# Moving the left output product and the second left V pass between the segments of a group in a recurrent-memory kernel

## The chip, the cores and the metric

The kernel runs on one core of one Trainium2 chip. The metric is the device time of one execution in microseconds (us), the lower the better. One profile was taken for each kernel.

## The reference, cut to what matters

The output is `x + A(xn) + B(xn)` with `xn` the layer norm of `x` (2048 rows of 1024). `B` is a dense GELU network and is not touched. `A` goes through 64 segments of 32 rows, one after the other, and carries 8 memory rows from each to the next:

```python
for s in range(n_seg):
    xs = x[:, s * seg_len:(s + 1) * seg_len, :].copy()
    h = jnp.concatenate([mem, xs], axis=1)             # 8 + 32 rows
    q = jnp.einsum('btd,dhe->bhte', h, Wq)             # 32 heads of 128
    k = jnp.einsum('btd,dhe->bhte', h, Wk)
    v = jnp.einsum('btd,dhe->bhte', h, Wv)
    # ... scaled scores, mask, softmax, p @ v ...
    o = jnp.einsum('bhte,hed->btd', o, Wo)
    mem = o[:, :M, :].copy()                           # 8 rows
    outs.append(o[:, M:, :])
```

## The kernel before

A segment has 40 rows, and this kernel gives TensorE tiles of 32 rows. So each segment's own pass takes the 8 memory rows and the first 24 (NX) rows of x. The last 8 (NL) rows, the "left" rows, need no memory for their projections, so they are done for four segments (a group, 4 x 8 = 32 rows) at once, as additional "left half passes" over weight slabs that are passing anyway. The left rows' attention outputs are gathered in `oL`, and their output product is taken once per group.

The weights are 64 slabs of 512 KB. Of these, 43 stay on the chip and 21 are streamed again in every segment through six buffers:

```python
NUNIT = 64
STREAMED = 21
STREAM_BUFS = 6
...
        def unit_done(unit):
            if IS_STREAMED[unit]:
                start_stream()          # the freed buffer is filled again
                ...                     # and a small transfer is issued
```

A half pass is 8 slabs: four matmuls of 512 columns for each slab, in four column tiles, and four more for the left rows where `left` says so. The output product has 16 slabs and eight matmuls of 256 columns for each.

```python
            more = g + 1 < NGRP
            left_k = i4 == 0                                      # K of this group, both halves
            left_q = first or (i4 == 2 and more)                  # Q of the next group
            left_v = first or (i4 == 3 and more), i4 == 0         # V, first and second half
            left_o = i4 == 3                                      # output product
```

So the four segments of a group carry 3, 0, 2 and 3 left half passes (the output product counts two). `qS` keeps the last segment's queries when the next group's replace them in PSUM:

```python
            def keep_q(u):
                nc.vector.tensor_copy(
                    out=qS[:, u, :, :], in_=by_head(qL[:, 4 * u:4 * u + 4, :])[:, :, 3 * NL:4 * NL]
                )
```

The end of a segment, with the load of `resL` (the left rows' residual) in the middle of the output product:

```python
                if n == 7:
                    res = sp.tile([P, 256], BF16, name="res", tag="e")
                    nc.gpsimd.dma_start(out=res[:, :], in_=hr_d[s + 1, :, 256:512])
                    if left_o:
                        resL = late.tile([P, 256], BF16, name="resL", tag="VL1")
                        nc.gpsimd.dma_start(out=resL[:, :], in_=hrL_d[g + 1, :, 256:512])
            ...
            if left_o:
                o_lefts(2)
                nc.vector.tensor_tensor(out=resL[:, :], in0=psXL[:, 0:256], in1=resL[:, :], op=ALU.add)
            if not final:
                put_mem(o_sb, nxt["hT"], trp.tile([P, 4, P], BF16, name="tr"))   # the memory copy, into hr
            nc.vector.tensor_tensor(out=res[:, :], in0=psX[:, 0:256], in1=res[:, :], op=ALU.add)
            # 4 stores of res, and in the fourth segment 16 of resL, go into a queue ("small")
```

`tag` names a buffer: tiles of the same tag share it, and a new one waits for the last reader of the old one. SBUF is full: 512 bytes more in a partition no longer fit.

The softmax here doesn't subtract the row's maximum and nothing guards it: scores larger than these inputs give would overflow.

## Time and profile before

| | before |
|---|---|
| median (3 runs) | 2343.41 us |
| TensorE, busy share | 87% |
| GB/s over the recurrent part, by slices of the span, without the last one | 359 to 406 |
| mean granted TensorE clock | 0.984 |
| longest waits of TensorE's matmuls, us in total | 50.8 for streamed Q slabs, 49.9 "issue" |

How to read the views: a row of a stretch gives its us, each engine's busy us with the count of instructions, the granted TensorE clock (1.00 is full), the transfer engines' busy share, and what they moved in GB/s. A wait row reads "who, tile, line <- whom it waited for: us in total, times, longest". The lines themselves stand in the prediction.

### The profile page before, as it was taken

The page shows a single profiled execution, that of the slowest core. Times are in us where ns is not written, and L with a number is a line of the kernel's source. Part 1 is how long each engine was busy: PE and PEld are TensorE (multiplying, and loading weights), DVE is VectorE, ACT ScalarE, POOL GpSimd, SP SyncE. Part 2 cuts the span into 40 slices and gives each one's busy share as a digit, 9 for nine tenths or more (in the row PEclk, how much of TensorE's full clock was granted, in tenths as well). Part 3 has the DMA queues.
Part 4 walks back from the last instruction along what each step waited for, and adds up shares of the span by engine and source line. Part 5 has one row for each costly group of instructions (what it writes and reads, how often), then busy time and mean ns, then how long its engine had stood idle before and what let it go on. Part 6 is the DMA issues. An engine that isn't in the chain of part 4 may idle for free.

```text
span 2342.5 us, 84620 instructions
## 1 busy us (share of the span) xinstructions
PE 2037.6 (87%) x37779; PEld 1052.9 (45%) x37779; DVE 698.9 (30%) x1922; ACT 516.9 (22%) x1221; POOL 372.7 (16%) x745
## 2 busy tenths in 40 slices
PE   7999999788888888888888888888888888888885
PEld 3444444344444544444444444444444444444443
DVE  6574753122222222222222222222222222222221
ACT  5261432121212121211121211111111111111121
POOL 0000000023121212121212121212121212121212
PEclk9999999999999999999999999999999999999998
DMA  9521126899999999999999999999999999999995
GB/s 326 186 68 47 39 67 256 331 400 372 405 376 404 383 399 374 403 369 389 377 405 367 388 366 404 365 402 367 406 372 404 368 399 361 399 370 403 375 405 225
DMA packets 266410, 792.03 MB, mean 338 GB/s; under 512 B 55996, under 2 KB 71132, under 8 KB 266045
## 3 DMA queue, kind: packets, MB, share of 16 engines
q1 hardware_dynamic: 243004, 769.66, 85.2%
q0 software_dynamic: 22464, 15.92, 2.2%
q8 instruction: 295, 4.83, 0.8%
q10 hardware_dynamic: 576, 1.05, 0.1%
q14 instruction: 71, 0.57, 0.1%
HBM read 772.83 MB, written 29.88 MB: 343 GB/s over the span
## 4 chain that ended last, share of the span: by engine, by line
PE 50%; DMA 40%; issue 4%; DVE 3%; ACT 2%; POOL 1%; DVEq 0%; ACTq 0%; POOLq 0%; SPq 0%
DMA u<-Wc_Q 24%; PE acc L536 18%; PE ps L358 8%; PE acc L676 8%; PE ps L405 6%; DMA u<-Wc_O 5%; DMA u<-Wc_V 4%; DMA u<-Wc_K 3%; PE av L654 2%; DMA resL<-hrL_d 2%; PE tr L493 2%; PE ps L438 2%; PE av L660 1%; DVE natL L564 1%; DVE pr L642 1%
## 5 line engine op out<-in xcount | busy, mean ns | idle before, releaser
L536 PE MATMUL acc<-u,hr 128*32 128x512 bf16 x12288 | 955.6, 385 | 128.7 <-DMA u<-Wc_Q 54.9
L536 PEld LDWEIGHTS <-hr 128*32 128x32 bf16 x12288 | 315.5, 96 | 469.7 <-issue 224.4
L536 PE MATMUL acc<-u,hrL 128*32 128x512 bf16 x3072 | 300.1, 383 | 4.3 <-issue 1.3
L559 ACT CAST nat<-acc 128x512 bf16<-128x512 f32 x256 | 149.8, 585 | 543.1 <-PE acc L536 504.8
L676 PEld LDWEIGHTS <-oT 128*32 128x32 bf16 x8192 | 210.5, 98 | 103.4 <-issue 80.9
L676 PE MATMUL acc<-u,oT 128*32 128x256 bf16 x4096 | 189.5, 277 | 27.0 <-issue 14.2
L564 DVE CAST natL<-acc 128x512 bf16<-128x512 f32 x224 | 152.5, 687 | 173.8 <-PE acc L536 173.8
L676 PE MATMUL acc<-W_O,oT 128*32 128x256 bf16 x4096 | 177.6, 283 | 30.4 <-issue 30.2
L358 PE MATMUL ps<-u 128*128 128x512 bf16 x896 | 195.8, 382 | 2.6 <-ACT u L282 2.6
L194 POOL DMA_DIRECT2D hr<-hr_d x63 | 35.0, 555 | 1009.6 <-PE acc L536 584.6
L778 POOL DMA_DIRECT2D out_dram<-res x256 | 129.4, 512 | 365.5 <-DVE res L774 362.3
L571 DVE COPY kT<-tr 128x512 bf16<-128x512 bf16 x128 | 54.4, 425 | 329.5 <-PE tr L493 329.5
L405 PE MATMUL ps<-u 128*128 128x512 bf16 x672 | 147.0, 379 | 0.0
L358 PEld LDWEIGHTS <-u 128*128 128x128 bf16 x896 | 88.0, 98 | 109.1 <-issue 4.5
L785 POOL DMA_DIRECT2D out_dram<-resL x256 | 127.9, 505 | 50.0 <-DMA out_dram<-resL 22.1
L628 ACT ACTIVATE pr<-sm 128x224 bf16<-128x224 f32 x128 | 45.7, 357 | 405.2 <-PE sm L623 337.3
L583 DVE COPY qT<-tr 128x512 bf16<-128x512 bf16 x128 | 54.4, 425 | 261.0 <-PE tr L493 261.0
L654 PEld LDWEIGHTS <-natL 32*128 32x128 bf16 x2048 | 78.8, 91 | 84.0 <-issue 50.3
L669 DVE CAST oT<-av 128x256 bf16<-128x256 f32 x128 | 54.4, 425 | 199.6 <-PE av L660 197.4
L536 PEld LDWEIGHTS <-hrL 128*32 128x32 bf16 x3072 | 84.2, 97 | 65.4 <-issue 11.3
L654 PE MATMUL av<-pr,natL 32*128 32x40 bf16 x2048 | 95.0, 177 | 17.3 <-DVE pr L642 9.5
L493 PEld LDWEIGHTS <-nat 128*128 128x128 bf16 x1024 | 57.9, 98 | 103.8 <-issue 60.1
(100 smaller groups left out, 1810.5 us busy)
## 6 DMA issues: line engine op xcount, KB each, us to landing
u<-Wc_K SPq DMA_DIRECT2D x384, 512.0 KB, 6.9
u<-Wc_Q SPq DMA_DIRECT2D x384, 512.0 KB, 7.3
u<-Wc_O SPq DMA_DIRECT2D x320, 512.0 KB, 7.3
u<-Wc_V SPq DMA_DIRECT2D x256, 512.0 KB, 6.6
u<-in_B_w_dram SPq DMA_DIRECT2D x16, 448.0 KB, 5.3
u<-in_B_w_dram SPq DMA_DIRECT2D x14, 512.0 KB, 10.7
u<-in_A_Wv_dram SPq DMA_DIRECT2D x12, 512.0 KB, 7.9
u<-in_A_Wk_dram SPq DMA_DIRECT2D x10, 512.0 KB
```

Of the source, the lines that this page charges most:

```text
L358: nc.tensor.matmul(ps[:, :].rearrange("p (s t) -> p s t", t=SEG), lhsT=w1_sb[fb // 14 * 8 + kt][:, (fb % 14) * P:(fb % 14 + 1) * P], rhs=x ...
L405: nc.tensor.matmul(ps[:, :], lhsT=gts[fc // 4][:, fc % 4, t * P:(t + 1) * P], rhs=w2_sb[fc // 2][:, fc % 2, cs], start=(fc == 0), stop=(fc ...
L493: nc.tensor.transpose(dst[:, c, :], nat[:, c * P:(c + 1) * P], ident[:, :])
L536: nc.tensor.matmul(acc[32 * j:32 * j + 32, :], lhsT=lhs[:, i, :], rhs=t[:, 512 * j:512 * j + 512], start=(i == seq[0]), stop=(i == seq[-1] ...
L559: nc.scalar.copy(out=nat[:, :], in_=ps[:, :])
L564: nc.vector.tensor_copy(out=nat[:, :], in_=psL[:, :])
L571: nc.vector.tensor_copy(out=st["kT"][:, :, :], in_=by_head(tr[:, :, :]))
L583: nc.vector.tensor_copy(out=st["qT"][:, :, 0:32], in_=by_head(tr[:, :, :]))
L654: nc.tensor.matmul(oV[:, b, c, :], lhsT=V[q, c * P:(c + 1) * P], rhs=prA[q, c, :], start=(c == 0), stop=False, skip_group_check=True, tile ...
L676: nc.tensor.matmul(acc[32 * jq:32 * jq + 32, 0:256], lhsT=lhs[i // 4][:, i % 4, 2 * u + k, :], rhs=t[:, 1024 * k + 256 * jq:1024 * k + 256 ...
L778: small.append(lambda o=o, r=res[32 * jq:32 * jq + NX, :]: nc.gpsimd.dma_start(out=o, in_=r))
L785: small.append(lambda o=o, r=r: nc.gpsimd.dma_start(out=o, in_=r))
```

## The change

Its intent is two left half passes in each segment, 2, 2, 2, 2 instead of 3, 0, 2, 3. The second left V goes from the first segment to the fourth. The left output product goes from the fourth to the second, and then covers the last four segments up to that one. To make this possible, `resL` leaves the buffer of VL1 for that of `qS`, and is loaded earlier. `keep_q(0)` and the transposes behind it go a little later, and stores are issued at once. The core, with cuts (`...`):

```diff
-            left_v = first or (i4 == 3 and more), i4 == 0
-            left_o = i4 == 3
+            left_v = first or (i4 == 3 and more)
+            left_o = i4 == 1 or final
+            og, slot = divmod(s + 2, GRP)
 ...
-                    at[5] = [lambda: turn_qL(st["natL"], 0)]
-                    ...
-                    qS = sp.tile([P, 2, 16, NL], BF16, name="qS")
-                    at[5].insert(0, lambda: keep_q(0))          # sixth slab of the first V pass
 ...
+            at = {1: [sums]}
+            if left_q and not first:
+                qS = sp.tile([P, 2, 16, NL], BF16, name="qS")
+                at[3] = [lambda: keep_q(0)]                     # fourth slab of the second K pass
+                at[5] = [lambda: turn_qL(st["natL"], 0)]
+            psK1, psK1L = half_pass("K", 1, left_k, at)
 ...
+                def load_resL():
+                    st["resL"] = sp.tile([P, 256], BF16, name="resL", tag="qS")
+                    nc.gpsimd.dma_start(out=st["resL"][:, :], in_=hrL_d[og, :, 256:512])
 ...
+                at[3].append(load_resL)
-            psV1, psV1L = half_pass("V", 1, left_v[1], at)
+            psV1, psV1L = half_pass("V", 1, left_v, at)
 ...
-                        small.append(lambda o=o, r=r: nc.gpsimd.dma_start(out=o, in_=r))
+                            nc.gpsimd.dma_start(out=out_flat[row:row + NL, cs], in_=resL[p0:p0 + NL, :])
```

More of the change, by code (lines that the diff above doesn't have):

```diff
@@ L311, in turn_R @@
             for i in range(4):
-                rows = R_n[ttg * P + i * SEG:ttg * P + (i + 1) * SEG, :].rearrange("t (j c) -> t j c", j=4)
-                dst = hr_d[4 * ttg + i + 1, :, 256:512].rearrange("(j t) c -> t j c", j=4)
-                dstL = hrL_d[ttg + 1, :, 256:512].rearrange("(j t) c -> t j c", j=4)[NL * i:NL * i + NL, :, :]
-                for o, r in ((dst, rows), (dstL, rows[NX:SEG, :, :])):
+                seg = 4 * ttg + i
+                rows = R_n[seg * SEG:(seg + 1) * SEG, :].rearrange("t (j c) -> t j c", j=4)
+                pairs = [(hr_d[seg + 1, :, 256:512].rearrange("(j t) c -> t j c", j=4), rows)]
+                og, slot = divmod(seg + 2, GRP)
+                for sl in (slot, slot ^ 2) if seg in (0, 1, NSEG - 2, NSEG - 1) else (slot,):
+                    dst = hrL_d[og, :, 256:512].rearrange("(j t) c -> t j c", j=4)[NL * sl:NL * sl + NL, :, :]
+                    pairs.append((dst, rows[NX:SEG, :, :]))
+                for o, r in pairs:
                     if small is None:
@@ L506 @@
         qL = qlp.tile([P, 8, P], BF16, name="qL")
-        kL, VL, oL = [None] * 2, [None] * 2, [None] * 2
+        kL, VL = [None] * 2, [None] * 2
+        oL = [late.tile([P, 4, 4, 32], BF16, name=f"oL{u}") for u in range(2)]
+        for t in oL:
+            nc.vector.memset(t[:, :, :, :], 0.0)
         for s in range(NSEG):
@@ L565, in left_out, with left_values @@
                 return nat
+            def left_values(u, ps):
+                VL[u] = left_out(ps, f"VL{u}", late)
             def turn_k(nat):
@@ L665, in values @@
                     st["oT", u] = sp.tile([P, 4, 4, 32], BF16, name="oT", tag="db"[u])
-                    if i4 == 0:
-                        oL[u] = late.tile([P, 4, 4, 32], BF16, name=f"oL{u}")
                 cp = nc.vector.tensor_copy if r else nc.scalar.copy
                 cp(out=st["oT", u][:, 2 * r:2 * r + 2, :, :], in_=oV[:, :, :, 0:32])
-                cp(out=oL[u][:, 2 * r:2 * r + 2, :, NL * i4:NL * i4 + NL], in_=oV[:, :, :, 32:40])
+                cp(out=oL[u][:, 2 * r:2 * r + 2, :, NL * slot:NL * slot + NL], in_=oV[:, :, :, 32:40])
             def o_product(unit, t, lhs, acc, seq):
@@ L698 @@
                 at[2].append(lambda: st.update(natL=left_out(psQL, "d")))
-                at[5] = [lambda: turn_qL(st["natL"], 0)]
                 if first:
-                    at[5].append(lambda: q_left(0))
-                else:
-                    qS = sp.tile([P, 2, 16, NL], BF16, name="qS")
-                    at[5].insert(0, lambda: keep_q(0))
-            psV, psVL = half_pass("V", 0, left_v[0], at)
+                    at[5] = [lambda: turn_qL(st["natL"], 0), lambda: q_left(0)]
+            psV, psVL = half_pass("V", 0, left_v, at)
             st["V"] = left_out(psV, "b")
             if first:
-                VL[0] = left_out(psVL, "VL0", late)
-            psK1, psK1L = half_pass("K", 1, left_k, {1: [sums]})
+                left_values(0, psVL)
+            at = {1: [sums]}
[4 more added lines that the diff above has]
+            psK1, psK1L = half_pass("K", 1, left_k, at)
             natk1 = rows_out(psK1, "d")
@@ L716 @@
                 at[4].insert(0, lambda: turn_kL(st["natL"], 1))
+            if left_v and not first:
+                at[6].append(lambda: left_values(0, psVL))
             psQ1, psQ1L = half_pass("Q", 1, left_q, at)
             natq1 = rows_out(psQ1, "b")
-            if left_v[0] and not first:
-                VL[0] = left_out(psVL, "VL0", late)
             at = {3: [lambda: turn_q(natq1)], 6: [lambda: scores(1)]}
@@ L734, in o_lefts @@
                         o_product(unit, unit_tile(unit), oL, psXL, O_LEFT_SEQ)
+                def load_resL():
+                    st["resL"] = sp.tile([P, 256], BF16, name="resL", tag="qS")
+                    nc.gpsimd.dma_start(out=st["resL"][:, :], in_=hrL_d[og, :, 256:512])
                 at.setdefault(1, []).append(lambda: o_lefts(0))
-            psV1, psV1L = half_pass("V", 1, left_v[1], at)
+                at[3].append(load_resL)
+            psV1, psV1L = half_pass("V", 1, left_v, at)
             st["V"] = left_out(psV1, "a")
-            if left_v[1]:
-                VL[1] = left_out(psV1L, "VL1", late)
+            if first:
+                left_values(1, psV1L)
             if not final:
@@ L745 @@
             at = {1: [sums], 4: [lambda: values(1, 0)], 6: [lambda: values(1, 1)]}
+            if left_v and not first:
+                at[6].append(lambda: left_values(1, psV1L))
             if left_q and not first:
@@ L750 @@
             psX = accp.tile([P, 512], F32, name="acc")
-            resL = None
             for n, unit in enumerate(O_UNITS):
@@ L762 @@
                     nc.gpsimd.dma_start(out=res[:, :], in_=hr_d[s + 1, :, 256:512])
-                    if left_o:
-                        resL = late.tile([P, 256], BF16, name="resL", tag="VL1")
-                        nc.gpsimd.dma_start(out=resL[:, :], in_=hrL_d[g + 1, :, 256:512])
             if not final:
@@ L770 @@
                 o_lefts(2)
+                resL = st["resL"]
                 nc.vector.tensor_tensor(out=resL[:, :], in0=psXL[:, 0:256], in1=resL[:, :], op=ALU.add)
@@ L776 @@
             for jq in range(4):
-                o = out_flat[s * SEG:s * SEG + NX, 256 * jq:256 * jq + 256]
-                small.append(lambda o=o, r=res[32 * jq:32 * jq + NX, :]: nc.gpsimd.dma_start(out=o, in_=r))
+                cs = slice(256 * jq, 256 * jq + 256)
+                nc.gpsimd.dma_start(out=out_flat[s * SEG:s * SEG + NX, cs], in_=res[32 * jq:32 * jq + NX, :])
             if left_o:
-                rows_o = out_flat[g * GRP * SEG:(g + 1) * GRP * SEG, :].rearrange("(i t) d -> i t d", t=SEG)
                 for jq in range(4):
-                    for i in range(GRP):
-                        o = rows_o[i, NX:SEG, 256 * jq:256 * jq + 256]
-                        r = resL[32 * jq + NL * i:32 * jq + NL * i + NL, :]
-                        small.append(lambda o=o, r=r: nc.gpsimd.dma_start(out=o, in_=r))
+                    cs = slice(256 * jq, 256 * jq + 256)
+                    for sl in range(GRP):
+                        row = (GRP * og - 2 + sl) * SEG + NX
+                        if s - GRP < row // SEG <= s and row >= 0:
+                            p0 = 32 * jq + NL * sl
+                            nc.gpsimd.dma_start(out=out_flat[row:row + NL, cs], in_=resL[p0:p0 + NL, :])
             if not final:
```

## The prediction

> **What bounds the kernel now.** I read the page from its second part, because a mean over the span hides the stages. The first seven of the 40 slices are the dense part, which the diff hardly touches. After them run 64 recurrent segments, which stream 21 of their 64 weight slabs (512 KB each) in every segment.
>
> ```profile
> DMA  9521126899999999999999999999999999999995
> GB/s 326 186 68 47 39 67 256 331 400 372 405 376 404 383 399 374 403 369 389 377 405 367 388 366 404 365 402 367 406 372 404 368 399 361 399 370 403 375 405 225
> ```
>
> The transfer engines look full everywhere, yet the rate swings between about 365 and 405 GB/s: something regular takes a tenth of it away. Segments go in groups of four, because work for the "left" 8 rows of four segments is batched, as extra "left half passes". One half pass is 8 slabs on TensorE. The segment ends are the copies that put the memory into hr; I cut one group at them. The columns are the stretch, its us, busy us by engine with counts, granted clock, DMA share and GB/s.
>
> ```profile
> 797.20:825.40 28.20, 25.85 (x572) 14.80 (x568) 8.50 (x24) 5.55 (x15) 11.65 (x23) 1.00 1.00 378
> 825.40:853.40 28.00, 22.38 (x476) 11.07 (x476) 6.03 (x19) 5.55 (x15) 3.12 (x6) 1.00 1.02 404
> 853.40:882.00 28.60, 26.05 (x548) 13.31 (x548) 7.43 (x22) 5.55 (x15) 3.11 (x6) 0.94 1.02 395
> 882.00:914.40 32.40, 28.04 (x648) 15.56 (x648) 6.82 (x21) 5.55 (x15) 3.64 (x7) 1.00 1.00 386
> ```
>
> By the code these carry 3 (K, K, one V), 0, 2 (Q, Q) and 3 (one V, and the output product, which is worth two) left half passes. The second has none and still takes 28.0 us at 404 GB/s: there the transfers are the bound. The fourth is the long one. Where does the rate go? The same view in short stretches across the group's end, at 914.4:
>
> ```profile
> 898.00:906.00 8.00, 7.48 (x198) 4.43 (x193) 2.82 (x8) 2.00 (x6) 0.55 (x1) 1.00 1.02 403
> 910.00:914.40 4.40, 2.40 (x58) 1.33 (x52) 0.50 (x3) 0.37 (x1) 0.00 (x0) 1.00 0.88 327
> 914.40:918.40 4.00, 3.92 (x71) 1.87 (x72) 0.35 (x2) 0.59 (x1) 3.36 (x7) 1.00 0.58 165
> 918.40:922.40 4.00, 3.86 (x63) 1.63 (x65) 2.00 (x5) 0.58 (x1) 2.22 (x6) 1.00 0.95 323
> ```
>
> There is one hole. All six stream buffers are full, since the fourth segment's TensorE work has outlasted the stream, and the next segment starts with slow K passes. Missing bytes against 404 GB/s: 77 x 4.4 + 239 x 4 + 81 x 4 = 1.62 MB, or 4.0 us. The group moves 28.2 x 378 + 28 x 404 + 28.6 x 395 + 32.4 x 386 = 45.8 MB, which at 404 GB/s takes 113.3 us, against 117.2 us: a gap of 3.9 us. So the hole is the whole of what better balance can win: about 15 x 3.9 = 58 us, 2.5%.
>
> Part of the hole is a wait on VectorE, in the wait view from 500 us on (total us, times, longest):
>
> ```profile
> DVE resL L771 <- DMA resL<-hrL_d: 59.2, 10, 7.0
> ```
>
> The add into resL waits for its load, and the memory copy, which the next segment needs, stands behind it.
>
> **What the Trainium skill says.** "DMA: Bandwidth & Descriptors", section Bandwidth, measures 425 GB/s for a 16 MB transfer and puts the port ceiling at 435; this trace shows 403 to 414 in full stretches, so 404 is a fair ceiling with the small transfers in. The same page, Anatomy of one DMA, says that the fixed cost of a transfer from GpSimd is mostly the wait for the write's receipt, 2.0 us in its fit. The trace agrees in kind but not in size: the 4 KB stores of resL take a median of 5.4 us to land under this load (1.5 at least). "Perfetto Trace Analysis", Optimization Strategy, says that regimes with different most-contended engines can gain from interleaving. The table above is that case. "TensorE: Matmul & The Clock Gate", part 3, says that column-tiled matmuls overlap in the array. Here groups of four start 0.21 to 0.22 us apart although one lasts 0.39:
>
> ```profile
> 1006.02 0.39 PE L536 MATMUL acc<-u,hrL 128*32 128x512 bf16 x4
> 1006.24 0.39 PE L536 MATMUL acc<-u,hr 128*32 128x512 bf16 x4
> 1006.45 0.39 PE L536 MATMUL acc<-u,hrL 128*32 128x512 bf16 x4
> ```
>
> So a left half pass costs 8 x 0.215 = 1.72 us of TensorE, and the left output product 3.44.
>
> **The change, part by part.** (1) V of the second half moves from the first segment to the fourth, the output product from the fourth to the second: 3, 0, 2, 3 becomes 2, 2, 2, 2. The instruction order adds only 128 matmuls (one output product, in the last segment), 3.4 us. The first segment, with three half passes, takes 28.2 us, of which TensorE's wait view gives 1.0 to streamed slabs; so three cost about 27.2 us and two about 25.5 (estimate). Four such make 102 us, below the 113.3 us of transfers: the kernel becomes bound by transfers throughout, and the hole should close.
>
> (2) resL is loaded during the V pass, not in the output product: the wait above (6.0 us idle on VectorE in this group, of which the next segment feels some 1.4) goes.
>
> (3) resL shares its buffer with qS, no longer with VL1. In the third segment keep_q(0) writes qS, so it must wait until all 16 stores of resL have landed. The instruction order shows that wait on keep_q, and a wait for VectorE on the qL transposes behind it. This is the new cost. How late do they land? The trace of before has the same 4 + 16 stores after its fourth segment, which ends at 914.4:
>
> ```profile
> 915.04 2.02 POOL L778 DMA_DIRECT2D out_dram<-res  x4 [6.10 <-DVE res L774]
> 917.05 1.99 POOL L785 DMA_DIRECT2D out_dram<-resL  x4
> 919.49 1.00 POOL L785 DMA_DIRECT2D out_dram<-resL  x2 [0.44 <-DMA out_dram<-res]
> 924.30 2.00 POOL L785 DMA_DIRECT2D out_dram<-resL  x4 [0.37 <-DMA out_dram<-resL]
> 926.97 1.14 POOL L785 DMA_DIRECT2D out_dram<-resL  x2 [0.67 <-DMA out_dram<-resL]
> ```
>
> The last is issued 13.2 us into the segment and lands near 18.4 (+5.4 is the median; the packets of 14 groups end at 18.4 on average). The author put keep_q(0) later, to the fourth slab of the second K pass, but TensorE gets to its transposes (two slabs on) 11.9 us into a third segment, averaged over 14 of them in the trace. So TensorE stands still for about 7 us in every third segment.
>
> (4) Stores go out at once instead of through the small queue. GpSimd issued them back to back before too, as shown; nothing changes but the tail. The last segment stores 8 pieces of resL instead of 16: 8 x 0.505 = 4.0 us, and about 0.6 us for the earlier resL.
>
> **What is hidden.** A TensorE stall costs nothing while the stream still has empty buffers. Six buffers of 512 KB at 404 GB/s are 7.8 us. By the time of the stall one or two may already be full, since the left output product lets the stream run ahead; so of 7 us, 0 to 1.5 us leave the transfers idle. After it TensorE starts with full buffers and at once meets the second left Q pass: 8 slabs take 3.44 us and transposes, against 8/3 x 1.3 = 3.5 us of transfers, so the stream pauses again for about 1 us. I take 1.9 us of idle in all: 115.2 us per group, 2.0 saved. Sum: 15 x 2.0 = 30 us in the groups, near 5 in the tail, and 2 to 3 for the first groups, whose s=2 stall is shorter (8 stores): 2343.4 - 37 = 2306.
>
> **Rivals.** A: the stall is wholly hidden (buffers are empty when it comes), and the hole closes: 58 + 5 saved, 2280. For it: by the trace the second segment is starved and so leaves the stream little ahead. Against it: the 7 us are close to all that the buffers hold. B: the stall takes the place of the hole in full, because the stores are slower under a stream that is now always saturated, or TensorE comes to it with several buffers full: 3.5 to 4 us idle per group, 2335 to 2340. For it: 5.4 us to landing is ruled by load, and up to eight stores are out at once, so each us more adds two over 16 stores. C: instruction fetches or small loads limit the rate: TensorE has unexplained stalls ("issue") of 1 to 1.7 us in output passes. These are there before as well and should cancel.
>
> **Range and chances.** 2306 us with 2276 to 2334 for 8 in 10: the low end is rival A at a slightly better rate, the high end near rival B. Faster by over 2% needs under 2297, that is 2.8 of the 3.9 us in each group: 0.34. Slower by over 2% would need a stall that outruns the buffers by 7 us: 0.02.
>
> **What would show it.** Right: four segments of nearly equal half passes, the resL wait gone, the 165 GB/s hole at the group's start gone, GB/s in the 40 slices near 395 and flat. For the stall: a new row "qL waits for qS" on TensorE of about 15 x 7 us, VectorE's qS waiting for out_dram<-resL, the third segment the longest (34 us) and the fourth and first short (24 to 26). The prediction is wrong if that row is missing or under 3 us each (then A), or if the rate in the third segment falls under 360 (then B).

## The result, and the profile after

| | before | after |
|---|---|---|
| median of 4 runs | 2346.33 us | 2482.95 us |
| lowest, highest | 2343.22, 2351.43 | 2467.62, 2486.84 |
| clock in the profiled run | 0.984 | 0.952 |

The ratio is 1.0568 (95% interval 1.0518 to 1.0618): slower by 5.7%, outside the predicted range. All ratios here are the mean time of one kernel's runs over that of the runs of the kernel before in the same rounds, so not quite the ratio of the medians quoted. The experiments ran on four chips, so the ratios are the safer comparison.

The page's second part, of the changed kernel (clock, busy share of the transfers in tenths, GB/s, in 40 slices):

```profile
PEclk9999999999898999998999899999998999999898
DMA  9422028999898989898989899989898999999996
GB/s 327 162 63 56 30 84 308 403 362 399 308 397 306 396 317 399 324 391 308 397 329 390 309 388 338 395 320 385 334 383 317 359 359 373 350 348 350 336 382 269
```

The swing has not gone. It has become deeper, to 306 GB/s, and the clock row now dips; in the kernel before, that row was nines up to the last slice. One group, cut at the copies into hr:

```profile
1204.10:1232.40 28.30, 25.06 (x548) 13.12 (x540) 8.02 (x22) 5.56 (x15) 3.11 (x6) 1.00 1.02 397
1232.40:1263.80 31.40, 25.40 (x604) 14.35 (x604) 6.35 (x21) 5.56 (x15) 4.16 (x8) 1.00 1.01 389
1263.80:1299.60 35.80, 25.92 (x548) 13.30 (x548) 7.44 (x23) 5.55 (x15) 11.11 (x22) 0.86 0.80 285
1299.60:1329.40 29.80, 25.29 (x548) 13.06 (x552) 7.15 (x21) 5.56 (x15) 3.11 (x6) 1.00 1.03 406
```

TensorE is nearly equally busy in all four, 25.1 to 25.9 us: the balance was reached. Yet the third segment takes 35.8 us. The waits that this was expected to show, from 500 us on:

```profile
PE qL L497 <- DVE qS L612: 100.5, 14, 8.5
DVE qS L612 <- DMA out_dram<-resL: 96.7, 13, 8.3
```

The stall is where the prediction put it, and as long: 100.5 us in 14 segments, 7.2 us each. The row of resL waiting for its load is gone from the list. The third segment and the end of the second, in short stretches:

```profile
1258.00:1263.80 5.80, 3.53 (x114) 2.85 (x106) 0.49 (x3) 0.37 (x1) 0.28 (x1) 1.00 0.90 328
1263.80:1267.80 4.00, 3.91 (x72) 1.86 (x74) 0.36 (x2) 0.59 (x1) 3.35 (x7) 1.00 0.81 275
1267.80:1274.80 7.00, 6.22 (x130) 2.90 (x130) 2.72 (x7) 1.52 (x4) 4.65 (x11) 1.00 1.01 386
1274.80:1278.80 4.00, 0.00 (x0) 0.00 (x0) 0.00 (x0) 0.00 (x0) 2.00 (x5) 0.65 1.03 405
1278.80:1282.30 3.50, 0.00 (x0) 0.00 (x0) 0.10 (x1) 0.00 (x0) 0.00 (x0) 0.50 0.33 126
1282.30:1286.30 4.00, 3.83 (x36) 1.40 (x35) 0.12 (x1) 0.59 (x1) 0.00 (x0) 0.51 0.36 129
1286.30:1294.30 8.00, 7.71 (x193) 4.05 (x190) 2.55 (x8) 2.00 (x6) 0.56 (x1) 1.00 0.79 245
```

Three things are to be seen. The hole after the left output product is still there (328 and 275 GB/s), one boundary earlier in the group than before. In the stall (no TensorE work at all) the transfers go on for 4 us and then run dry (126). And after the stall they stay low for 12 us, while TensorE is busy: for the first 4 us its clock is 0.51, then 1.00. TensorE's list in order of time shows that clock in the distance between groups of four matmuls:

```profile
1284.67 0.64 PE L547 MATMUL acc<-u,hr 128*32 128x512 bf16 x4
1285.10 0.64 PE L547 MATMUL acc<-u,hrL 128*32 128x512 bf16 x4
1285.52 0.64 PE L547 MATMUL acc<-u,hr 128*32 128x512 bf16 x4
...
1286.97 0.39 PE L547 MATMUL acc<-u,hrL 128*32 128x512 bf16 x4
1287.18 0.39 PE L547 MATMUL acc<-u,hr 128*32 128x512 bf16 x4
```

They start 0.42 to 0.43 us apart at first and 0.21 later. Against 404 GB/s, the bytes missing from the dry part of the stall to the segment's end are 278 x 3.5 + 275 x 4 + 159 x 8 + 49 x 5.3 (that last stretch ran at 355) = 3.6 MB, or 8.9 us. Over 15 groups that is 134 us, and the kernels differ by 137.

### The profile page after: what moved, and what is told of

The parts are those of the page before. It is cut to its first block, busy times and chain, and to the rows that moved or that the text cites. A ratio compares the mean times of both kernels' runs of the same rounds, so it can differ in the third digit from the quotient of the medians.

```text
span 2485.1 us, 84860 instructions
## 1 busy us (share of the span) xinstructions
PE 2067.6 (83%) x37907; PEld 1063.8 (43%) x37907; DVE 701.0 (28%) x1925; ACT 517.4 (21%) x1221; POOL 374.2 (15%) x748
## 4 chain that ended last, share of the span: by engine, by line
DMA 35%; PE 35%; issue 5%; DVE 3%; ACT 2%; POOL 2%; DVEq 0%; ACTq 0%; POOLq 0%; SPq 0%
PE acc L547 17%; DMA u<-Wc_Q 16%; PE acc L688 9%; DMA out_dram<-res 5%; DMA out_dram<-resL 5%; PE av L668 2%; DMA res<-hr_d 2%; PE tr L497 2%; DMA u<-Wc_O 2%; DMA u<-Wc_V 2%; DMA u<-Wc_K 1%; POOL out_dram L795 1%; PE av L674 1%; POOL out_dram L803 1%; DVE pr L656 1%
## 5 line engine op out<-in xcount | busy, mean ns | idle before, releaser
L547 PE MATMUL acc<-u,hr 128*32 128x512 bf16 x12288 | 979.4, 395 | 113.7 <-DMA u<-Wc_Q 36.4
L547 PE MATMUL acc<-u,hrL 128*32 128x512 bf16 x3072 | 310.0, 396 | 9.4 <-ACT nat L570 7.8
L688 PE MATMUL acc<-W_O,oT 128*32 128x256 bf16 x4096 | 180.9, 288 | 30.4 <-issue 30.2
L547 PEld LDWEIGHTS <-hrL 128*32 128x32 bf16 x3072 | 87.1, 100 | 84.9 <-issue 30.4
L497 PE MATMUL qL<-ident,natL 128*128 128x128 bf16 x128 | 16.2, 266 | 112.6 <-DVE qS L612 108.8
```

The costliest lines, as they stand in the source:

```text
L497: nc.tensor.transpose(dst[:, c, :], nat[:, c * P:(c + 1) * P], ident[:, :])
L547: nc.tensor.matmul(acc[32 * j:32 * j + 32, :], lhsT=lhs[:, i, :], rhs=t[:, 512 * j:512 * j + 512], start=(i == seq[0]), stop=(i == seq[-1] ...
L688: nc.tensor.matmul(acc[32 * jq:32 * jq + 32, 0:256], lhsT=lhs[i // 4][:, i % 4, 2 * u + k, :], rhs=t[:, 1024 * k + 256 * jq:1024 * k + 256 ...
```

## The experiments

The means by segment below were worked out by cutting each trace at the copies into hr, without the first group.

| kernel | median, us | ratio to before | 1st | 2nd | 3rd | 4th | group |
|---|---|---|---|---|---|---|---|
| before | 2346.3 | 1 | 28.5 | 27.9 | 28.8 | 32.2 | 117.4 |
| after | 2482.95 | 1.0568 | 28.9 | 32.5 | 36.4 | 29.0 | 126.8 |
| e1_staged_store | 2346.17 | 1.0002 | 28.5 | 32.3 | 28.2 | 28.6 | 117.6 |
| e2_before_early_resL | 2341.79 | 0.9985 | 28.8 | 28.0 | 28.6 | 31.6 | 117.0 |
| e5_V1_in_first | 2338.04 | 0.9972 | 29.3 | 31.9 | 27.9 | 27.7 | 116.8 |
| e3_filler_in_stall | 2450.45 | 1.0445 | 28.5 | 32.5 | 34.6 | 28.7 | 124.3 |
| e7_half_the_stores | 2408.63 | 1.0256 | 28.3 | 32.3 | 32.8 | 28.9 | 122.3 |
| e6_half_left_product | 2326.87 | 0.9917 | 28.0 | 31.5 | 28.9 | 28.2 | 116.6 |
| e8_wide_left_product | 2319.53 | 0.9885 | 27.8 | 31.5 | 28.4 | 28.2 | 115.9 |
| v1_split_left_product | 2335.28 | 0.9949 | 31.2 | 27.8 | 28.9 | 28.7 | 116.6 |
| e10_no_left_product | 2301.16 | 0.9816 | 28.5 | 28.4 | 29.0 | 29.0 | 114.9 |
| e9_five_buffers | 2445.23 | 1.0410 | 30.6 | 33.3 | 29.4 | 29.9 | 123.1 |
| v2_wide_left_product | 2320.19 | 0.9875 | 29.3 | 30.4 | 28.5 | 27.5 | 115.7 |

e6, e8 and e10 compute wrong left rows; their result still passed the comparison on the chip, whose tolerance is coarse beside the attention's share of the output. e7 leaves half of the left rows unwritten. The third segment of the last group has no left Q pass and so no stall; it is in the means of the 3rd column.

### e1: take the cause of the stall away

The buffer cannot get a tag of its own, since SBUF is full. So resL goes out in one store to a scratch tensor, and the 16 pieces are put in place from there.

```diff
+    oL_d = dram.tile([NGRP + 1, P, 256], BF16, name="oL_d")
 ...
+            if left_o:
+                nc.gpsimd.dma_start(out=oL_d[og, :, :], in_=resL[:, :])
 ...
-                            nc.gpsimd.dma_start(out=out_flat[row:row + NL, cs], in_=resL[p0:p0 + NL, :])
+                            nc.gpsimd.dma_start(out=out_flat[row:row + NL, cs], in_=oL_d[og, p0:p0 + NL, :])
```

> The changed kernel, but resL goes to a scratch tensor in one store, and the 16 pieces are put in place from there, so its buffer is free after one landing (about 8 us into the third segment, before keep_q needs it at about 10.6). Theory S (the loss is the stall on the shared buffer and what follows it: per group 4.6 us of idle transfers in the stall and 4.6 after it, by the 1-us rate table of the changed kernel; balance itself wins nothing, because the hole of 4.0 us after the left output product only moved): the row of qL waiting for qS falls from 7.5 us per group to under 0.5, and the time to 2483 - 15 x 9.2 = 2345, ratio to before 0.99 to 1.01. Rival B (balance works as I predicted, the hole goes): 2280 to 2300, ratio 0.98 or less. Rival O (direct stores or the output product in the second segment are slow in themselves): stays over 2390, ratio over 1.02.

Measured: 2346.17 us, ratio 1.0002 (0.9984 to 1.0020). The wait of qL for qS is 1.1 us in all. So the whole 5.7% is the stall and what follows it, and all the rest of the change, the balance included, is worth nothing within 0.2% (e1's own extra store is in this sum and was not measured apart). The stretches around the end of a second segment show why (it ends at 1218.1):

```profile
1212.20:1218.10 5.90, 3.60 (x118) 2.91 (x106) 0.53 (x3) 0.37 (x1) 0.34 (x1) 1.00 0.94 341
1218.10:1222.10 4.00, 3.95 (x72) 1.90 (x76) 0.33 (x1) 0.59 (x1) 2.69 (x6) 1.00 0.90 297
1222.10:1229.10 7.00, 6.37 (x133) 3.05 (x133) 2.86 (x8) 1.52 (x4) 4.90 (x10) 1.00 1.01 386
```

It is the hole of before, at the segment that now has the output product, although that segment has no other left work and the next begins with plain K passes.

### e2: the early load of resL alone

The kernel before, with `load_resL` in the V pass of the fourth segment, into the buffer of qS (free there).

> The kernel before, with resL loaded during the V pass instead of the output product (into qS's buffer, whose last reader is by then done and whose next writer comes three segments later, so no stall). Takes the early load alone. Theory S: the wait of the memory copy behind the resL add (about 1.4 us per group) goes, but part of it is under the same hole, so 10 to 20 us faster, ratio 0.991 to 0.996. Rival H (the hole is made by the output product alone and the wait is hidden in it): no change, ratio 0.998 to 1.002.

Measured: 2341.79 us, ratio 0.9985 (0.9969 to 1.0002). resL no longer waits for its load, but the gain, if there is one, is about 4 us, less than the 10 to 20 expected. The whole interval lies above theory S's 0.991 to 0.996, so theory S fell as it was put; the interval also reaches 1, so a gain is not shown, and more than 7 us is excluded. That fits a wait that was mostly inside the hole.

### e5: where the left V stands

```diff
-            psV1, psV1L = half_pass("V", 1, left_v, at)
+            psV1, psV1L = half_pass("V", 1, i4 == 0, at)
```

> As e1_staged_store, but the left V of the second half stays in the first segment: 3, 2, 2, 1 left half passes instead of 2, 2, 2, 2. Theory S (where V stands hardly matters, because only the time of the left output product fills the stream buffers): within 0.5% of e1_staged_store. Rival B (equal loads are what counts): slower than e1_staged_store by 1.7 us per group, 25 us, 1.1%.

Measured: 2338.04 us, 0.3% under e1. Loads of 3, 2, 2, 1 do as well as 2, 2, 2, 2 (the intervals, 0.9944 to 1.0001 and 0.9984 to 1.0020, overlap). Equal loads by segment are not what counts.

### e3: the clock apart from the stall

```diff
+                def filler():          # into an unused PSUM tile, never read
+                    av = avp.tile([P, 2, 512], F32, name="av")
+                    t = res_tiles["K", 1, 1]
+                    for n in range(32):
+                        for j in range(4):
+                            nc.tensor.matmul(
+                                av[32 * j:32 * j + 32, 0, :], lhsT=hT[:, 1, :], rhs=t[:, 512 * j:512 * j + 512],
+                                start=True, stop=True, tile_position=(0, 32 * j),
+                            )
+
+                at[4] = [filler]
                 at[5] = [lambda: turn_qL(st["natL"], 0)]
```

> The changed kernel with 32 groups of four matmuls (6.9 us, into an unused PSUM tile, never read) in front of the transposes that wait for qS, so TensorE works through most of the stall instead of standing still. Results stay right. Theory C (the idle stall drops TensorE's granted clock to 0.5 for about 4 us after it, and that costs 2 us per group): the clock stays at 1.0 after the stall, mean clock back near 0.98, and the time falls by about 30 us to 2450, ratio 1.045. Rival N (after the stall the stream, not the clock, sets the pace): the time stays within 10 us of 2483 or rises.

Measured: 2450.45 us, mean clock 0.986. Useless work in the stall makes the kernel 32 us faster than leaving TensorE idle, 2.2 us per group. The stretches from the start of a third segment:

```profile
1254.60:1265.40 10.80, 10.71 (x205) 4.92 (x209) 3.08 (x9) 2.10 (x5) 7.52 (x16) 1.00 0.93 343
1265.40:1272.90 7.50, 6.67 (x124) 3.58 (x117) 0.00 (x0) 0.00 (x0) 2.49 (x5) 1.00 0.73 285
1272.90:1276.90 4.00, 3.20 (x56) 1.53 (x55) 0.65 (x2) 0.58 (x1) 0.00 (x0) 1.00 0.34 120
1276.90:1284.90 8.00, 7.63 (x214) 4.31 (x208) 2.25 (x7) 2.49 (x8) 0.56 (x1) 1.00 0.91 294
```

The clock stays at 1.00, but the transfers still run dry and stay low. The remaining 104 us over e1, 7.0 us per group, are no matter of the clock. (The filler does not lengthen the wait much: the transposes come 19.1 us into a third segment on average, against 18.7 in the changed kernel and 11.6 in e1.) The Trainium skill states the clock's rule ("TensorE: Matmul & The Clock Gate", Part 1): a TensorE that is idle for a window of about 3.4 us is throttled to half its clock, and needs as long of work to get it back. After 7.2 us of standing still the clock is 0.51 for 4 us, and the low stretches of the traces last 3.41, 6.83 or 10.24 us. But 3.4 us of idle time is no limit here: in the kernel before, none of its matmuls waits for more than 2.7 us between 500 and 2300 us, and yet its clock is halved 14 times there, for 3.41 us each. My prediction left the clock out.

### e7: half the stores

```diff
-                    for sl in range(GRP):
+                    for sl in range(2):
```

> The changed kernel with 8 of the 16 pieces of resL stored per group (half of the left rows are not written: wrong result on purpose). By the pace of the stores before (0.68 us each) the last of 8 lands near 12.5 to 13 us into the third segment, so TensorE waits about 2 us instead of 7.5. Theory S (a stall costs only what the full stream buffers cannot cover,[...]): of the 137 us lost more than three quarters come back, 2350 to 2375 us, ratio 1.00 to 1.015. Rival L (loss is proportional to the stall): 137 x 2/7.5 remain, 2383, ratio 1.016 or more.

Measured: 2408.63 us, ratio 1.0256 (1.0214 to 1.0297). TensorE's wait for qS:

```profile
PE qL L497 <- DVE qS L612: 47.4, 14, 5.8
```

The stall is 3.4 us in the mean, not the 2 that I expected, and 62 us of the loss remain, 4.2 us per group. Theory S fell here: far less than three quarters came back. The sum looks proportional, as rival L has it (3.4 / 7.2 x 137 = 65), but this is in part luck, since the clock's share did not shrink with the stall. Theory S had also taken it that so short a stall leaves the clock alone. It doesn't. After a stall of 3.1 us, which ended at 1126.3:

```profile
1125.90:1129.60 3.70, 3.26 (x32) 1.39 (x35) 0.22 (x1) 0.59 (x1) 0.00 (x0) 0.54 1.03 396
```

In all 14 third segments the clock is halved for a time, although in 7 of them no wait of the matmuls is longer than 3.3 us. TensorE works at half clock for 5.2 us in each of them on average, against 4.9 in the changed kernel and 0.9 in e3. If that costs the 2.2 us per group of the changed kernel, some 2 us of the 4.2 are left for the stall of 3.4 itself (an estimate). So the buffers cover up to about 1.4 us of the short stall, and next to nothing of the long one: 7.0 us of cost, with the clock held, for 7.2. A run of e7 with the clock held was not made.

### e6 and e10: how much of the hole is the left output product

In both, only some of the 16 units of the left product are taken, on e1: in e6 the five streamed ones and the last three, in e10 the last one.

```diff
+        O_LEFT = [], [unit for unit in O_UNITS if IS_STREAMED[unit]], O_UNITS[-3:]     # e6
+        O_LEFT = [], [], O_UNITS[-1:]                                                  # e10
```

> e1_staged_store with 8 of the 16 units of the left output product (wrong result on purpose): takes 1.72 us of TensorE out of the second segment and nothing else. Theory H (the hole of about 4 us of idle transfers comes from the left output product standing in one piece at the end of a segment, and it is what six buffers cannot cover): the hole shrinks by as much as is taken out or more, 1.7 to 3.5 us per group, 2294 to 2320 us, ratio 0.978 to 0.989. Rival T (the hole is the chain at the segment's end or the resL add, not the product): within 10 us of e1_staged_store, ratio over 0.996.

> e1_staged_store with 1 of the 16 units of the left output product (wrong result on purpose): the second segment has then almost no left work, 2, 0, 2, 2. Theory H (the hole at the end of the second segment is made by the left output product): all of it goes, 113 to 114 us per group, 2285 to 2305 us, ratio 0.974 to 0.982; the low rates at the second segment's end and the third's start (under 350 GB/s) rise to about 380. Rival T (chain at the segment's end, output transfers, instruction fetches of the main product): over 2320, ratio over 0.988.

Measured: e6 2326.87 us, outside the expected 2294 to 2320 (1.3 us per group for 1.72 us of matmuls); e10 2301.16 us, 45 us under e1's median, or 3.0 us per group for 15 x 0.215 = 3.2 us of matmuls. These matmuls come with waits: in e1 the whole product takes 5.0 us on average, from the first matmul of each of its pieces to the next piece of other work. So e10 takes out some 4.7 us and wins 3.0. Work in this place costs most of its length, although the segment's transfers take longer than its TensorE work. In e10 the hole is gone, at the same place as above (a second segment ends at 1189.3):

```profile
1183.30:1189.30 6.00, 4.18 (x127) 3.02 (x119) 1.07 (x4) 0.86 (x3) 0.53 (x1) 1.00 1.03 400
1189.30:1193.30 4.00, 3.88 (x67) 1.92 (x67) 0.42 (x1) 0.59 (x1) 2.40 (x5) 1.00 1.03 406
1193.30:1200.30 7.00, 6.69 (x133) 3.02 (x131) 2.52 (x7) 1.52 (x4) 4.36 (x10) 1.00 1.03 410
```

### e8: the same columns with half the instructions

On e1, the left product takes two halves of 512 columns for each head instead of four quarters of 256 (even heads in partitions 0 to 63, odd ones in 64 to 127, which are not added up: wrong).

> e1_staged_store with the left output product in 512-wide matmuls, 4 per unit instead of 8 (wrong result on purpose; the same columns stream through TensorE, with half the instructions). Theory H (columns): no change, within 10 us of e1_staged_store, ratio 0.996 to 1.004. Rival F (part of the hole is TensorE waiting for instructions, the row acc waits for issue with 1.7 to 2.8 us in that segment): 1 to 2 us per group less, 2316 to 2331, ratio 0.987 to 0.994.

Measured: 2319.53 us, 27 us under e1, with nearly unchanged matmul time (a unit beside the main product takes 0.219 us in e1 and 0.216 here, medians from its first matmul to the next instruction). So the number of instructions has a part in it. TensorE's "issue" row for the output products, of e1 first:

```profile
PE acc L689 <- issue: 55.1, 44, 2.6
```

and of e8, where the main product has L702:

```profile
PE acc L702 <- issue: 34.4, 33, 2.0
```

Summed over every row in which TensorE's matmuls wait for "issue", it is 75.6 us in e1 and 62.3 in e8. That explains half of the 27 us at most; the other half stays open. The Trainium skill ("Runtime: NRT & Kernel Launch", Instruction fetch mechanics) says that instructions are fetched in 16 KiB blocks by an own queue, and that crossing a block is mostly hidden. e1's trace has this queue with 296 packets of 16 KB; TensorE's 75814 instructions are 296 blocks of 256, the page's size of a block. Between 500 and 2300 us, 50 of its "issue" waits last over 0.5 us (70.3 us in all), and every one of them ends 1.26 to 1.63 us after one of these packets has ended, where 7 in 100 moments taken at random lie 1.2 to 1.7 us behind one. So these waits end with a fetch, and beside a saturated stream fetches are not hidden here. That the stream is what makes them late is not shown.

### v1: the left product cut in two

Five streamed units and three at the end stay in the first segment, the other eight go into the Q and V passes of the second, which has no other left work.

```diff
+        DEFER = [unit for unit in O_UNITS[:-3] if not IS_STREAMED[unit]]
+        NOW = [], [unit for unit in O_UNITS if IS_STREAMED[unit]], O_UNITS[-3:]
 ...
+            split = s > 0 and i4 == 0
+            left_o = split or s == 1 or final
+            og, slot = divmod(s + 3, GRP)
```

> A version meant to beat both (right result). The left output product is cut in two: in the first segment of a group only the 5 streamed units beside the main product and 3 at the end, the other 8 units (1.72 us) in the Q and V passes of the second segment, which has no other left work. V as in the changed kernel (fourth), keep_q where it was before, resL kept from the first to the second segment, where nothing else needs its buffer. Theory H: no stall, and the hole shrinks from 4 us to 0 to 1.5: 114 to 115.5 us per group, 2290 to 2315 us, ratio 0.977 to 0.987. Rival B' (any uneven load, here 3, 1, 2, 2 half passes, brings its own hole): 2335 to 2350, ratio 0.996 to 1.003.

Measured: 2335.28 us, ratio 0.9949 (0.9913 to 0.9984). It is correct and a little faster than before, and a miss against 2290 to 2315, at the lower end of rival B': its first segment, with two left K passes and half of the product, takes 31.2 us and has a hole of its own (253 GB/s at the lowest just after its end, in 1 us slices, mean of 14 groups).

### e9: the size of the window

```diff
-STREAM_BUFS = 6
+STREAM_BUFS = 5
```

> e1_staged_store with five stream buffers instead of six (one more slab stays where the sixth was; the same slabs are streamed). Theory W (what counts is how much TensorE work stands within the window of the stream buffers, some 18 of 64 slabs, not within a segment): every hole grows by what one buffer holds, 1.3 us or more per group, and others open: 2366 to 2410 us, ratio 1.008 to 1.027. Rival (the window does not matter as long as a segment's work is under its transfer time): within 0.4% of e1_staged_store.

Measured: 2445.23 us, 99 us over e1 (96 by the ratios), more than expected. Every segment gets longer, by 1.0 to 2.1 us, while no segment's work or bytes have changed. So the number of buffers sets how far TensorE and the transfers hold each other up. How much of it is the window and how much the shorter queue of transfers in flight, this run doesn't tell.

### v2: a version that beats both

e5 with the wide left product made right: a copy to SBUF, then eight matmuls with parts of the identity add the odd and even heads in the next segment's first K pass, in front of one staged store.

```diff
+                def fold(natXL=natXL, resL=resL, og=og, s=s):
+                    psS = accp.tile([P, 512], F32, name="acc")
+                    for k in range(2):
+                        for jq in range(4):
+                            q = 64 * k + 32 * (jq // 2)
+                            nc.tensor.matmul(
+                                psS[32 * jq:32 * jq + 32, 0:256], lhsT=ident[:, q:q + 32],
+                                rhs=natXL[:, 256 * (jq % 2):256 * (jq % 2) + 256],
+                                start=(k == 0), stop=(k == 1), tile_position=(0, 32 * jq),
+                            )
+                    nc.vector.tensor_tensor(out=resL[:, :], in0=psS[:, 0:256], in1=resL[:, :], op=ALU.add)
```

> A version meant to beat both (right result): e5_V1_in_first with the left output product in 512-wide matmuls (4 per unit instead of 8, even heads in partitions 0 to 63 and odd heads in 64 to 127), folded by 8 matmuls of 256 columns in the next segment's first K pass, then one staged store. Theory F (the instruction stream is part of the hole: e8 won 27 us against e1 with it): 2305 to 2320 us, ratio 0.982 to 0.989. Rival: the fold and the copy in front of it (0.7 us on VectorE, 0.2 us on TensorE) cost what the wide matmuls win: ratio 0.995 to 1.0.

Measured: 2320.19 us, ratio 0.9875 (0.9854 to 0.9897): 1.2% faster than before. The hole at the end of its second segment (1198.5) is smaller, with 399 and 346 GB/s where e1 had 341 and 297:

```profile
1192.60:1198.50 5.90, 4.57 (x122) 3.28 (x120) 0.77 (x4) 0.37 (x1) 0.53 (x1) 1.00 1.03 399
1198.50:1202.50 4.00, 3.97 (x76) 2.00 (x76) 1.33 (x3) 0.58 (x1) 2.57 (x5) 1.00 0.96 346
```

v1 and v2 passed the comparison on the chip. It is coarse, since e6, e8 and e10 passed it too.

## Why the prediction was wrong

- **The stall was right** in its place, its cause, its chain of waits and its length: "about 7 us in every third segment", measured 7.2. (Its list of stores leaves out two rows, with 4 of the 16.) The shared buffer of qS and resL is the cause; e1 takes it away and the 137 us with it.
- **"Six buffers of 512 KB at 404 GB/s are 7.8 us [...] so of 7 us, 0 to 1.5 us leave the transfers idle"** is the step that cost most. I took 1.9 us of idle per group in all; the stall alone cost 7.0 with the clock held (e3 against e1) and 9.1 without, and the hole of 4 us came on top. The transfers ran on for 4 us, not 7.8: some buffers were already full or in use. And the buffers that the stall fills are then missing for what follows. In e1 the stream carries about 400 GB/s through the passes after this point (1 us slices, mean of 14 groups), where after a stall it carries 129 and then 245. So a stall of 7.2 us is not hidden but counts nearly one for one; of the 3.4 us in e7 some 2 remain once the clock's share is taken off (an estimate). That the full buffers are the reason is my reading of those rates; the costs themselves are measured.
- **The clock was not in the prediction.** The stall leaves TensorE at half its clock for the first 4 us of work, 2.2 us per group more (e3), and stalls of 3 us did so too (e7).
- **"Four such make 102 us, below the 113.3 us of transfers: the kernel becomes bound by transfers throughout, and the hole should close"** failed as well. The 102 us were right (101.7 busy in the group shown), the loads became equal, and the hole stayed: 1.0002 for e1, and e5 with unequal loads is no slower. The first and fourth segments took 28.9 and 29.0 us, not the 24 to 26 expected. Sums over a segment of 28 us don't tell, because TensorE and the stream are tied together over six buffers, some 8 us. The left output product stands in the last 14 us of a segment (five of its 16 units together, eight beside the main product, three at the end), and there it costs most of its length (e10: 3.0 us won for 3.2 us of matmuls and their waits). Moving it moves the hole.
- **The early load of resL was right** as to the wait, but was worth about 4 us in all, if anything, and 7 at most (e2).
- **The tail and the stores** were right in kind and too small to see beside the rest.
- **Rival B**, the stall in the hole's place, had the right direction, but reckoned 3.5 to 4 us for a stall and hole together that were 9 and 4.

## What to carry to other kernels

When engines and a stream are tied together by a few buffers, balance the work over the time that these buffers hold, not over a loop body; a body's sums can be equal and every hole still there. Count a long stall in front of a busy stretch at its full length, and add what TensorE's clock loses after it, which here did not shrink when the stall was halved. Before a tile is put into the buffer of another, look up when the last store of it lands, not when it is issued.

## What the Trainium skill lacked or had wrong

- "Runtime: NRT & Kernel Launch", Instruction fetch mechanics, calls instruction fetches mostly hidden. Beside a stream at about 400 GB/s, TensorE's matmuls waited 75.6 us for "issue" in e1, up to 2.6 us at once, all but 5.3 us of it in waits that end with a fetch, and halving the instructions of one product won 27 us (2346.17 to 2319.53), half of it at most through these waits. The page has no word on fetches beside saturated transfers.
- "DMA: Bandwidth & Descriptors", Anatomy of one DMA, has a fixed cost of 2.0 us. The 4 KB stores here took 5.4 us in the median beside the stream and 1.5 at least, and 16 of them in a row needed some 18 us until the last had landed. (The page does say, under Latency and other measured facts, that load raises the latency of the memory, to 2 us.)
- "TensorE: Matmul & The Clock Gate", Part 1, names an idle window of about 3.4 us for the half clock. Here shorter idle times did it as well: 14 times between 500 and 2300 us in the kernel before, whose matmuls never waited more than 2.7 us there, and after a stall of 3.1 us in e7.
- No page says that stream buffers do not hide a stall of TensorE when a TensorE-heavy stretch follows it: a stall of 7.2 us cost 7.0 us with the clock held and 9.1 us without, with six buffers that hold 7.8 us of transfers.
